# Hashed attention with a three-way maxout layer: weight tiles added by VectorE in three bursts of the first batch, the fourth pair's hash one unit earlier, and two end pieces

## The chip, the cores and the metric

One core of a Trainium2 chip runs the whole kernel. The metric is the device time of one launch in microseconds. Times inside the kernel are counted from the start of the profiled span.

## The reference, cut to what matters

```python
# q, k, v: 4 batches x 8 heads x 768 rows x 64; proj: 64 x 6
q_bucket = bucket of the 6 signs of q @ proj ; k_bucket likewise
scores = where(q_bucket[:, None] == k_bucket[None, :], 0.125 * q @ k.T, -1e9)
attn = exp(scores - max);  attn = attn / (sum(attn) + 1e-9);  x = attn @ v
# x: 3072 rows x 512 (the heads side by side)
h = maximum(maximum(x @ w1, x @ w2), x @ w3)      # 512 -> 768
out = h @ w_out                                   # 768 -> 512, float32
```

Each row's weights are divided by their sum. How that sum is formed is what the first part of the change touches.

## The kernel before, in words

**Units.** The work is cut into chunks of query rows: three of 256 rows in batch 0, two of 384 in each other batch, nine in all (0 to 8). A unit is a part of one chunk and one head: 768 scores per partition, three blocks of 256 or two of 384. A chunk and head has two units in batch 0 and three later, so each batch has 48 units. In batch 0 the order of units is: chunks 0, 1, 2 for head 0, the same for head 1, then heads 2 and 3 of each chunk in turn, then heads 4 to 7 of chunk 0 (units 24 to 31), of chunk 1 and of chunk 2.

For each unit, `scores` (line 289) issues TensorE matmuls of keys against queries (line 305) into one of two PSUM buffers, and one ScalarE exponential (line 313) into one of 24 weight tiles `AT`. Bits of the hash stand as extra rows of the matmul operand `S`, so that unequal buckets get a weight of almost nothing.

**Bursts.** A burst is one chunk and one half of the heads, written (chunk, half): (1, 0) is chunk 1 with heads 0 to 3. It has three pieces. `sums` (line 358) adds the weights over the keys: matmuls against a 128 x 32 matrix of ones (line 365), four heads side by side; VectorE turns the sums into reciprocals in four steps (lines 372 to 376, `ys`, `rr`, `rr`, `rb`). `values` (line 378) multiplies the weights with `v`, once for even and once for odd columns (line 387), and VectorE scales the result into `xT` (line 394). In chunks 3 to 8 VectorE first adds a head's weight tiles (`add`, line 329), so that fewer matmuls are needed in `sums`; in chunks 0 to 2 all six blocks of a head go through TensorE, 24 matmuls a burst.

**Order.** Nothing is left to a scheduler. Every engine runs its instructions in the order in which the program issues them, and waits where an operand or a buffer isn't there. The loop at line 624 issues, for unit `u`: the scores of unit `u + 1`, then whatever `when(u, ...)` has listed for `u`, then ffn steps as the credit allows, then pieces of bursts. The bursts of batch 0 have units of their own:

```python
u = {(0, 0): (16, 17, 20), (1, 0): (21, 22, 24), (2, 0): (26, 27, 29)}.get((c, i), (d, d, d))[n]
```

Burst (0, 1) has `d = 32` for its three pieces. The ffn of chunk 0 starts two units later; its first matmuls (line 420) need all of that chunk's `xT`.

**Hash.** For the heads of batch 0 by pairs: a transposing matmul (line 123), copies into `T`, GpSimd's scaled copy into `S` (line 137), the projection matmul, and VectorE's sign bits (line 153). For pairs 2 and 3 (`pair_hash`, line 145; pair 2 is the third and pair 3 the fourth) four small DMAs carry the bits into `S`: key side and query side of two heads. Pair 3 is hashed at unit 18; its key bits are sent by SyncE at once, its query bits by ScalarE's queue at unit 20. Pair 3 is first used by unit 28.

For later batches VectorE transposes four loaded heads (line 209), GpSimd narrows them to 16 bits (line 214), SyncE places them (line 219), and the hash (lines 228 to 239) sends its bits. The transposes of the first such group stand at units 22 to 29, one each.

**End.** The last block of 128 output rows is written in pieces, `last` (line 441): TensorE matmuls (line 445), a copy by ScalarE or VectorE (lines 449, 451), a DMA by that engine's queue or SyncE's (line 453).

Of the kernel before, what the change touches and what calls it, by code (L numbers as in the profile page):

```python
# [10 lines left out]
FP16 = mybir.dt.float16  # L11
BF16 = mybir.dt.bfloat16
AluOp = mybir.AluOpType
# [4 lines left out]
def kernel(  # L18
# [12 lines left out]
    nc = tc.nc  # L31
    B, H, S, D = q.shape
    NBITS = proj.shape[1]
    P = 128
    NM = S // P
    HALF = S // 2
    MH = NM // 2
    DM = H * D
# [14 lines left out]
    NAT = 24  # L53
    SPREAD = {2: (61, 9), 3: (100, 12)}
    THIRD_ADD = 5
    LAG = (1, 4)
    ATW = 776

# [8 lines left out]
    ad_pool = ctx.enter_context(tc.tile_pool(name="adpool", bufs=5))  # L67
# [22 lines left out]
    def bank():  # L90
        i = free_banks.pop(0)
        return i, bank_tiles[i]

    def give(i):
        if i is not None:
            free_banks.append(i)


    nat, t32, t16, s_of, where, v_at = {}, {}, {}, {}, {}, {}
# [42 lines left out]
        pair_keep(pi, side, hd, mp, eng)  # L142
        give(i)

    def pair_hash(pi, late=None):
        i, bp = bank()
        for side in (1, 0):
            for hd in range(2):
                g = 2 * side + hd
                nc.tensor.matmul(bp[Q * g : Q * (g + 1), 0:HALF], pj2[:, :],  # L150
                                 t32[pi][:, side, hd * HALF : (hd + 1) * HALF], start=True, stop=True)
        bits = b_pool.tile([P, HALF], BF16, tag="bits", name="bits")
        nc.vector.tensor_scalar(out=bits[:], in0=bp[:, 0:HALF], scalar1=0.0, scalar2=0.5,
                                op0=AluOp.is_gt, op1=AluOp.subtract)
        give(i)

        def send(eng, sides):
            for hd in range(2):
                for side in sides:
                    g = 2 * side + hd  # L160
                    eng.dma_start(s_of[pi][D : D + NBITS, g, :].rearrange("b (c n) -> b c n", c=2),
                                  bits[Q * g : Q * g + 2 * NBITS, :])

        if late:
            send(nc.sync, (1,))
            when(late, send, nc.scalar, (0,))
        else:
            send(nc.sync, (1, 0))


    def first_place(side, hd, par, mp):
# [101 lines left out]
    done_at = {}  # L273
# [8 lines left out]
    def blocks(t, w):  # L282
        nb = 2 * HALF // w
        return t[:, 0 : nb * (w + 2)].rearrange("p (n c) -> p n c", n=nb)

    def block_of(b, m):
        return 2 * (m % MH) + m // MH if b == 0 else m
# [29 lines left out]
    def weights_of(c, h, m):  # L317
        w = chunks[c][2]
        nb = 2 * HALF // w
        return blocks(at_tiles[at_of[unit_at[c, h, m // nb]]], w)[:, m % nb, :]  # L320

    def xt_of(c):
        if c not in xts:
            xts[c] = x_pool.tile([P, NJC, HALF], FP16, tag="xT", name="xT")
        return xts[c]

    sum_of = {}

    def add(c, h, n):
        w = chunks[c][2]  # L330
        t = [blocks(at_tiles[at_of[unit_at[c, h, i]]], w)[:, :, 0:w] for i in range(n + 1)]
        if n == 1:
            sum_of[c, h] = ad_pool.tile([P, 2, HALF], FP16, tag="ad", name="ad")
        else:
            t[0] = sum_of[c, h][:]
        nc.vector.tensor_tensor(out=sum_of[c, h][:], in0=t[0], in1=t[n], op=AluOp.add)  # L336
        if n == 2 and c >= THIRD_ADD:
            t = sum_of[c, h]
            nc.vector.tensor_tensor(out=t[:, 0, :], in0=t[:, 0, :], in1=t[:, 1, :], op=AluOp.add)  # L339

    def sum_blocks(c, h):
        w = chunks[c][2]
        if (c, h) in sum_of:
            t = sum_of[c, h]
            return [t[:, j, 0:w] for j in range(1 if c >= THIRD_ADD else 2)]
        return [weights_of(c, h, m)[:, 0:w] for m in range(NM)]

    def burst(c, i):
# [60 lines left out]
    def ffn_groups(c):  # L409
        b, q0, w = chunks[c]  # L410
        xt = xt_of(c)
        hts, gs, l2 = {}, [], {}
        jobs = [(fb, wi) for fb in range(NFB) for wi in range(3)]
        if c == 0:
            jobs = [(fb, wi) for wi in range(3) for fb in range(NFB)]
        for fb, wi in jobs:
            def go(fb=fb, wi=wi):
                k_, ps = bank()
                for jc in range(NJC):
                    nc.tensor.matmul(ps[:, 0:w], w_sb[wi][:, jc, fb * P : (fb + 1) * P], xt[:, jc, 0:w],  # L420
                                     start=(jc == 0), stop=(jc == NJC - 1))
                if wi == 0:
                    hts[fb] = h_pool.tile([P, HALF], FP16, tag="ht", name="ht")
                    if w == HALF:
                        nc.scalar.copy(hts[fb][:, 0:w], ps[:, 0:w])  # L425
                    else:
                        nc.vector.tensor_copy(hts[fb][:, 0:w], ps[:, 0:w])
                else:
                    nc.vector.tensor_tensor(out=hts[fb][:, 0:w], in0=hts[fb][:, 0:w], in1=ps[:, 0:w], op=AluOp.max)  # L429
                give(k_)  # L430
            gs.append(go)
        rows = out[b * S : (b + 1) * S, :].rearrange("(p c) m -> c p m", c=NM)

        def out_rows(tb):
            if c < NCH - 1:
                return o_pool.tile([P, DM], FP32, tag="osb", name="osb")
            if "end" not in nat:
                nat["end"] = nat_pool.tile([P, 4 * NM * D], FP32, tag="nat", name="nat")
            return nat["end"][:, tb * DM : (tb + 1) * DM]

        def last(tb, cs, use_act):
            k_, ps = bank()
            n = cs.stop - cs.start
            for fb in range(NFB):
                nc.tensor.matmul(ps[:, 0:n], hts[fb][:, tb * P : (tb + 1) * P], wout_sb[:, fb, cs],
                                 start=(fb == 0), stop=(fb == NFB - 1))
            osb = out_rows(tb)
            if use_act:
                nc.scalar.copy(osb[:, cs], ps[:, 0:n])
            else:  # L450
                nc.vector.tensor_copy(osb[:, cs], ps[:, 0:n])
            give(k_)
            (nc.scalar if use_act else nc.sync).dma_start(rows[block_of(b, q0 // P + tb)][:, cs], osb[:, cs])

        def item(tb, part):
            def go2(part, tb=tb):
                if c == NCH - 1 and tb == w // P - 1:
                    if part == 0:
                        last(tb, slice(0, DM // 2), False)
                    else:  # L460
                        last(tb, slice(DM // 2, 3 * DM // 4), True)
                        last(tb, slice(3 * DM // 4, DM), False)
                    return
                if part == 0:
                    l2[tb] = bank()
                k_, ps = l2[tb]
                for fb in range(part * MH, (part + 1) * MH):
                    nc.tensor.matmul(ps[:, 0:DM], hts[fb][:, tb * P : (tb + 1) * P], wout_sb[:, fb, :],  # L468
                                     start=(fb == 0), stop=(fb == NFB - 1))
                if part == 1:  # L470
                    osb = out_rows(tb)
                    nc.scalar.copy(osb[:, 0:DM], ps[:, 0:DM])  # L472
                    give(k_)
                    nc.sync.dma_start(rows[block_of(b, q0 // P + tb)], osb[:, 0:DM])
            gs.append(lambda: go2(part))

        ntb = w // P
        steps = [(0, 0)]
        for tb in range(1, ntb):
            steps += [(tb, 0), (tb - 1, 1)]  # L480
        steps.append((ntb - 1, 1))
        if c == NCH - 1:
            steps = steps[:-3] + [steps[-2], steps[-3], steps[-1]]
        for tb, part in steps:
            item(tb, part)
        return gs
# [3 lines left out]
    def when(u, f, *args):  # L490
        at.setdefault(u, []).append(lambda: f(*args))

    with tc.manual_schedule():
# [80 lines left out]
        when(9, t32.pop, 1)  # L574
        when(14, pair_hash, 2)
        when(15, t32.pop, 2)
        when(18, pair_hash, 3, 20)
        when(19, t32.pop, 3)
        when(17, load_v, 1)
        for n, u in ((1, 6), (2, 20), (3, 31)):  # L580
            when(u, load_weights, n)
# [4 lines left out]
        for g in range(2, NQUAD):  # L586
            b2, i2 = divmod(g, 2)
            need = UPB * b2 + 12 * i2
            for n, side in enumerate((1, 0)):
                name = (side, g)  # L590
# [17 lines left out]
        for c, i in sorted(done_at, key=lambda e: done_at[e]):  # L608
            d = done_at[c, i] + LAG[c > 2]
            sums, values = burst(c, i)  # L610
            pieces = [lambda f=sums: f(0, NM), lambda f=values: f(0, 0, NM), lambda f=values: f(1, 0, NM)]
            for n, f in enumerate(pieces):
                u = {(0, 0): (16, 17, 20), (1, 0): (21, 22, 24), (2, 0): (26, 27, 29)}.get((c, i), (d, d, d))[n]
# [6 lines left out]
        for u, (c, h, n) in enumerate(units):  # L620
            if c >= 3 and n:
                when(min(u + 2, NU - 1), add, c, h, n)

        for u in range(NU):
            if 0 < u < NU - 1:
# [55 lines left out]
```

## Time and profile before

| what | value |
|---|---|
| median of 3 runs | 265.78 us (265.35 to 266.68) |
| the profiled execution | 265.72 us, span 263.3 us |
| TensorE matmul, weight load | 256.2 us (97%), 154.2 us (59%) |
| VectorE, ScalarE, GpSimd | 208.4 us (79%), 177.4 us (67%), 69.9 us (27%) |
| TensorE's granted clock | 1.0 |
| sums without adds (line 365, 128 x 256) | 144 matmuls, 24 in each burst |
| adds of two weight tiles (line 336) | 48, mean 545 ns |

A timeline line gives start and length in microseconds, the engine, line and operation, output and inputs, shapes, how many instructions are merged in it, and in brackets the idle time before it with what ended it. A `q` behind an engine's name means its queue issues a DMA. A line of busy times by stretch gives the stretch, its length, then for TensorE, weight load, VectorE, ScalarE and GpSimd the busy time and number of instructions, then the granted clock, DMA share and GB/s. A group of instructions has its busy time, the mean length in ns and the idle time before it. Lines refer to the kernel as shown.

### The profile page before, as it was taken

What the parts mean: (1) busy time and instruction counts of PE and PEld (TensorE: products, weight loads), DVE (VectorE), ACT (ScalarE), POOL (GpSimd) and SP (SyncE); (2) the same over time, 40 slices, a digit from 0 to 9 for tenths busy, and PEclk for the clock granted to TensorE, in tenths of its full rate; (3) what the DMA queues carried; (4) which work ended last, traced back from release to release, by engine and by line L of the source; (5) the groups of instructions that cost most, each with busy time, mean ns of one, the idle gap of its engine ahead of it and who ended that gap; (6) DMA issues with size and microseconds to landing.
All of it is one profiled execution on the core that took longest, in us unless ns stands there. A gap on an engine that the chain in (4) does not pass through costs nothing.

```text
span 263.3 us, 6497 instructions
## 1 busy us (share of the span) xinstructions
PE 256.2 (97%) x2509; PEld 154.2 (59%) x2509; DVE 208.4 (79%) x494; ACT 177.4 (67%) x257; POOL 69.9 (27%) x132
## 2 busy tenths in 40 slices
PE   7999999999999999999999999999999999999994
PEld 3555658866765666555555554655555555554552
DVE  3897767967799999969999996999859795887451
ACT  3697785667968675956869588584886859581322
POOL 5587752355043526330141612011000000000000
PEclk9999999999999999999999999999999999999999
DMA  6998999869732964970063753802030003000303
GB/s 199 301 247 176 193 256 236 167 118 209 191 91 65 207 143 62 267 185 21 0 193 108 121 120 52 206 0 70 7 123 0 0 2 121 2 0 2 120 0 120
DMA packets 20861, 30.95 MB, mean 118 GB/s; under 512 B 2624, under 2 KB 15392, under 8 KB 20832
## 3 DMA queue, kind: packets, MB, share of 16 engines
q0 software_dynamic: 8128, 13.37, 27.0%
q1 hardware_dynamic: 12156, 16.71, 21.8%
q10 hardware_dynamic: 548, 0.48, 0.7%
q8 instruction: 19, 0.31, 0.5%
q14 instruction: 10, 0.08, 0.1%
HBM read 25.17 MB, written 6.29 MB: 119 GB/s over the span
## 4 chain that ended last, share of the span: by engine, by line
PE 84%; DVE 7%; POOL 3%; issue 1%; DMA 1%; ACT 1%; ACTq 0%; DVEq 0%
PE ms L420 34%; PE sc L305 21%; PE ms L468 11%; PE ms L387 9%; PE ms L228 3%; PE ms L365 2%; POOL S L137 2%; DMA nat<-in_q_dram 1%; DVE S L183 1%; PE ms L123 1%; PE ms L178 1%; DVE ht L429 1%; DVE T L132 1%; DVE ad L336 1%; DVE xT L394 1%
## 5 line engine op out<-in xcount | busy, mean ns | idle before, releaser
L313 ACT ACTIVATE AT<-sc 128x768 f16<-128x768 f32 x192 | 152.7, 816 | 59.6 <-PE sc L305 54.9
L420 PE MATMUL ms<-xT,w_sb 128*128 128x384 f16 (+1 forms) x648 | 115.0, 307 | 0.3 <-DVE xT L394 0.2
L305 PE MATMUL sc<-S 72*128 72x384 bf16 (+1 forms) x432 | 93.9, 308 | 1.6 <-ACT AT L313 0.7
L420 PEld LDWEIGHTS <-w_sb 128*128 128x128 f16 x648 | 62.7, 97 | 35.9 <-issue 0.4
L429 DVE TENSOR_TENSOR ht<-ht,ms 128x384 f16<-128x384 f16 (+1 forms) x108 | 54.2, 503 | 20.8 <-PE ms L420 10.3
L305 PEld LDWEIGHTS <-S 72*128 72x128 bf16 (+1 forms) x432 | 39.4, 98 | 32.7 <-issue 11.9
L214 POOL TENSOR_SCALAR T<-T 128x768 bf16<-128x768 f32 x24 | 22.9, 952 | 90.3 <-issue 48.3
L468 PE MATMUL ms<-wout_sb,ht 128*128 128x512 f16 x138 | 35.5, 378 | 0.0
L387 PE MATMUL ms<-AT,vo 128*32 128x385 f16 (+3 forms) x840 | 34.3, 308 | 0.0
L387 PEld LDWEIGHTS <-vo 128*32 128x32 f16 x864 | 22.9, 96 | 9.2 <-issue 1.7
L336 DVE TENSOR_TENSOR ad<-ad,AT 128x768 f16<-128x768 f16 x48 | 26.5, 552 | 2.1 <-ACT AT L313 1.3
L209 DVE STREAM_TRANSPOSE T<-nat 128x384 f32<-128x384 f32 x48 | 26.8, 563 | 0.0
L336 DVE TENSOR_TENSOR ad<-AT,AT 128x768 f16<-128x768 f16 x48 | 26.2, 545 | 0.2 <-ACT AT L313 0.2
L425 ACT CAST ht<-ms 128x384 f16<-128x384 f32 x36 | 17.3, 480 | 8.1 <-PE ms L420 8.1
L468 PEld LDWEIGHTS <-ht 128*128 128x128 f16 x138 | 13.3, 97 | 13.0 <-issue 0.3
L394 DVE SCALAR_TENSOR_TENSOR xT<-ms,sv,rb 128x384 f16<-128x384 f32 (+1 forms) x35 | 19.2, 566 | 1.4
L472 ACT COPY osb<-ms 128x512 f32<-128x512 f32 x21 | 12.3, 587 | 7.1 <-PE ms L468 5.8
L339 DVE TENSOR_TENSOR ad<-ad 128x384 f16<-128x384 f16 x32 | 15.5, 485 | 1.1
L137 POOL TENSOR_SCALAR S<-T 64x384 bf16<-64x384 f32 (+1 forms) x23 | 14.2, 617 | 5.8 <-DVE T L132 4.3
L203 POOL DMA_DIRECT2D nat<-in_q_dram x20 | 11.1, 560 | 0.1
L372 DVE STREAM_TRANSPOSE ys<-ms 128x384 f32<-128x384 f32 (+1 forms) x17 | 9.0, 530 | 2.4 <-PE ms L365 2.3
L183 DVE TENSOR_SCALAR S<-ms 6x384 bf16<-6x384 f32 x16 | 8.9, 554 | 2.4 <-PE ms L178 2.0
(52 smaller groups left out, 122.0 us busy)
## 6 DMA issues: line engine op xcount, KB each, us to landing
out_dram<-osb SPq DMA_DIRECT2D x21, 256.0 KB
S<-T SPq DMA_DIRECT2D x48, 96.0 KB
nat<-in_q_dram POOLq DMA_DIRECT2D x20, 192.0 KB, 6.4
vo<-in_v_dram POOLq DMA_DIRECT2D x8, 384.0 KB, 6.1
nat<-in_k_dram POOLq DMA_DIRECT2D x16, 192.0 KB, 5.8
w_sb<-in_moe_w_dram POOLq DMA_DIRECT2D x3, 768.0 KB, 12.0
nat<-in_k_dram SPq DMA_DIRECT2D x10, 192.0 KB
nat<-in_k_dram SPq DMA_DIRECT2D x3, 384.0 KB
```

The lines of the kernel that those rows point to most:

```text
L137: nc.gpsimd.tensor_scalar(out=o, in0=i_, scalar1=RS, scalar2=1.0, op0=AluOp.mult, op1=AluOp.mult)
L209: nc.vector.transpose(t32[name][:, u, half * HALF : (half + 1) * HALF], i_)
L214: nc.gpsimd.tensor_scalar(out=t16[name][:, u, :], in0=t32[name][:, u, :], scalar1=RS, scalar2=1.0, op0=AluOp.mult, op1=AluOp.mult)
L305: nc.tensor.matmul(views[j], s_of[kn][0 : D + bits, kx, m * P : (m + 1) * P], s_of[qn][0 : D + bits, qx, q0 : q0 + w], start=True, stop=True)
L313: nc.scalar.activation(t[:, :, 0:w], whole, ActFn.Exp, bias=-SCALE * 0.25 * bits, scale=SCALE)
L336: nc.vector.tensor_tensor(out=sum_of[c, h][:], in0=t[0], in1=t[n], op=AluOp.add)
L387: nc.tensor.matmul(av[Q * x : Q * (x + 1), 0:n], v_at[2 * b + i][:, x, cb * D + side : (cb + 1) * D : 2], weights_of(c, 4 * i + x, m)[:, 0 ...
L394: nc.vector.scalar_tensor_tensor(out=xt_of(c)[:, 2 * i + side, 0:w], in0=av[:, 0:w], scalar=sv_of[b, i, side][:], in1=rb[0][:, 0:w], op0=A ...
L420: nc.tensor.matmul(ps[:, 0:w], w_sb[wi][:, jc, fb * P : (fb + 1) * P], xt[:, jc, 0:w], start=(jc == 0), stop=(jc == NJC - 1))
L425: nc.scalar.copy(hts[fb][:, 0:w], ps[:, 0:w])
L429: nc.vector.tensor_tensor(out=hts[fb][:, 0:w], in0=hts[fb][:, 0:w], in1=ps[:, 0:w], op=AluOp.max)
L468: nc.tensor.matmul(ps[:, 0:DM], hts[fb][:, tb * P : (tb + 1) * P], wout_sb[:, fb, :], start=(fb == 0), stop=(fb == NFB - 1))
```

## The change

Three edits. VectorE adds the two weight tiles of each head in the bursts (1, 0), (2, 0) and (0, 1): twelve adds more, and 12 instead of 24 matmuls in the sums of each of the three. The adds stand at units 17, 17, 19, 20 for (1, 0), ahead of its sums at 21; at 22, 22, 23, 24 for (2, 0), ahead of 26; at 27, 29, 31, 32 for (0, 1), ahead of 32. In a unit, an add comes behind the transpose of that unit and ahead of a burst's pieces. The fourth pair's hash moves from unit 18 to 17, which puts its matmuls ahead of the values of (0, 0) instead of behind block 19, and all four of its bit DMAs go to SyncE. The last output block is written in two pieces of 256 columns (ScalarE's copy and queue, then VectorE's copy and SyncE's queue) instead of pieces of 256, 128 and 128 (VectorE, ScalarE, VectorE).

```diff
+    ADDED = ((1, 0), (2, 0), (0, 1))
+    ADD_FROM = {(0, 1): 17, (0, 2): 22, (1, 0): 0, (1, 1): 0, (1, 2): 0}
...
-    def pair_hash(pi, late=None):
+    def pair_hash(pi):
...
-        def send(eng, sides):
-            for hd in range(2):
-                for side in sides:
-                    g = 2 * side + hd
-                    eng.dma_start(s_of[pi][D : D + NBITS, g, :].rearrange("b (c n) -> b c n", c=2),
+        for hd in range(2):
+            for side in (1, 0):
+                g = 2 * side + hd
+                nc.sync.dma_start(s_of[pi][D : D + NBITS, g, :].rearrange("b (c n) -> b c n", c=2),
                                   bits[Q * g : Q * g + 2 * NBITS, :])
-
-        if late:
-            send(nc.sync, (1,))
-            when(late, send, nc.scalar, (0,))
-        else:
-            send(nc.sync, (1, 0))
...
         if n == 1:
-            sum_of[c, h] = ad_pool.tile([P, 2, HALF], FP16, tag="ad", name="ad")
+            ad = ad_pool.tile([P, 2, HALF], FP16, tag="ad", name="ad").rearrange("p a c -> p (a c)")
+            sum_of[c, h] = ad.rearrange("p (n c) -> p n c", c=w)
         else:
-            t[0] = sum_of[c, h][:]
-        nc.vector.tensor_tensor(out=sum_of[c, h][:], in0=t[0], in1=t[n], op=AluOp.add)
+            t[0] = sum_of[c, h]
+        nc.vector.tensor_tensor(out=sum_of[c, h], in0=t[0], in1=t[n], op=AluOp.add)
...
-            return [t[:, j, 0:w] for j in range(1 if c >= THIRD_ADD else 2)]
+            return [t[:, j, :] for j in range(1 if c >= THIRD_ADD else 2 * HALF // w)]
...
                 if c == NCH - 1 and tb == w // P - 1:
-                    if part == 0:
-                        last(tb, slice(0, DM // 2), False)
-                    else:
-                        last(tb, slice(DM // 2, 3 * DM // 4), True)
-                        last(tb, slice(3 * DM // 4, DM), False)
+                    last(tb, slice(part * DM // 2, (part + 1) * DM // 2), part == 0)
                     return
...
-        when(18, pair_hash, 3, 20)
-        when(19, t32.pop, 3)
+        when(17, pair_hash, 3)
+        when(18, t32.pop, 3)
...
             if c >= 3 and n:
                 when(min(u + 2, NU - 1), add, c, h, n)
+            if (c, h // 4) in ADDED and n:
+                when(min(max(u + 2, ADD_FROM[h // 4, c]), done_at[c, h // 4] + 1), add, c, h, n)
```

## The prediction

> **What bounds the kernel now.** I read the page first: busy times and the chain that ended last.
>
> ```profile
> PE 256.2 (97%) x2509; PEld 154.2 (59%) x2509; DVE 208.4 (79%) x494; ACT 177.4 (67%) x257; POOL 69.9 (27%) x132
> PE 84%; DVE 7%; POOL 3%; issue 1%; DMA 1%; ACT 1%; ACTq 0%; DVEq 0%
> ```
>
> TensorE carries 84% of the chain, so its work looks worth removing. But the change lies in one stage, and the span's shares say nothing of it. Hence the busy times of the stretch with the three changed bursts, then its timelines, TensorE first.
>
> ```profile
> 29.00:41.00 12.00, 11.31 (x221) 7.22 (x221) 8.82 (x22) 9.07 (x12) 5.95 (x12) 1.00 1.08 226
> ```
> ```profile
> 28.18 0.84 PE L365 MATMUL ms<-AT,ones 128*32 128x256 f16 x24
> 33.01 0.85 PE L365 MATMUL ms<-AT,ones 128*32 128x256 f16 x24
> 37.99 0.49 PE L305 MATMUL sc<-S 70*128 70x256 bf16 x3 [0.34 <-ACT AT L313]
> 39.73 0.84 PE L365 MATMUL ms<-AT,ones 128*32 128x256 f16 x24
> 40.39 1.52 PE L387 MATMUL ms<-AT,vo 128*32 128x257 f16 x48
> 43.19 0.27 PE L420 MATMUL ms<-xT,w_sb 128*128 128x256 f16 x1 [0.19 <-DVE xT L394]
> ```
>
> The L365 rows are the sums that the change halves. After 43.19 the next row with a wait is at 81.36 (0.14 us), so what is late at 43.19 is late at the end. That row waits for VectorE. VectorE's timeline:
>
> ```profile
> 30.00 0.45 DVE L376 STREAM_TRANSPOSE rb<-rr 128x256 f32<-128x256 f32 x1
> 30.37 0.54 DVE L209 STREAM_TRANSPOSE T<-nat 128x384 f32<-128x384 f32 x1
> 30.83 0.44 DVE L394 SCALAR_TENSOR_TENSOR xT<-ms,sv,rb 128x256 f16<-128x256 f32 x1
> 31.19 1.02 DVE L209 STREAM_TRANSPOSE T<-nat 128x384 f32<-128x384 f32 x2
> 33.91 0.45 DVE L372 STREAM_TRANSPOSE ys<-ms 128x256 f32<-128x256 f32 x1 [0.22 <-PE ms L365]
> 39.98 0.56 DVE L231 TENSOR_SCALAR bits<-ms 128x384 bf16<-128x384 f32 x1 [2.56 <-PE ms L228]
> 40.61 0.45 DVE L372 STREAM_TRANSPOSE ys<-ms 128x256 f32<-128x256 f32 x1
> ```
>
> From 29.07 to 40.61 VectorE is idle only 0.22 + 2.56 = 2.78 us. That is all the cover the adds have there. Last, ScalarE at the moved DMA issues, then a place where an add meets GpSimd:
>
> ```profile
> 27.13 1.42 ACTq L161 DMA_DIRECT2D S<-bits  x1
> 28.59 0.74 ACTq L161 DMA_DIRECT2D S<-bits  x1
> 29.38 3.17 ACT L313 ACTIVATE AT<-sc 128x768 f16<-128x768 f32 x4 [1.13 <-PE ms L365]
> ```
> ```profile
> 84.63 0.51 DVE L336 TENSOR_TENSOR ad<-AT,AT 128x768 f16<-128x768 f16 x1
> 85.25 0.99 DVE L336 TENSOR_TENSOR ad<-ad,AT 128x768 f16<-128x768 f16 x1
> ```
> ```profile
> 84.86 0.99 POOL L214 TENSOR_SCALAR T<-T 128x768 bf16<-128x768 f32 x1 [2.55 <-issue]
> ```
>
> The second add starts while GpSimd narrows and ends 0.40 after it (85.84 to 86.24), 0.44 longer than its group's 0.55. The narrowing that met the first add took 0.99, not 0.83.
>
> **The change, part by part.** Times below are starts. "Block n" is the score matmuls of unit n; a burst is (chunk, half of the heads).
>
> *Fourth hash one unit earlier.* Today values of (0,0) lie between blocks 18 and 19 and the hash between 19 and 20; afterwards both lie between 18 and 19. A score block ahead of another kind takes 0.43 (23.76 to 24.20), values 0.78 (24.20 to 24.98), the hash 0.78 (25.42 to 26.20). Block 19 then starts at 25.76, not 24.98; its exponential 0.54 later (24.98 to 25.52 today) and 0.81 long, to 27.11. Block 21 needs the score buffer that this frees (there are two): 27.16, not 26.54. Sums (1,0) follow at 28.80, not 28.18: **+0.62**.
>
> *Sums halved.* 24 matmuls take 0.66 (39.73 to 40.39); 12 fewer save **0.33** a burst. After sums (1,0) TensorE is 0.29 late, and VectorE's first step of that burst is at 29.36 instead of 29.07.
>
> *Query-side bits to SyncE.* ScalarE loses two issues. Exponential 22 starts at 28.91 instead of 29.38 and block 24 no longer waits (0.21 today). TensorE is at 30.49 there against 30.44: level again. SyncE gets two issues of 0.72; its four now run from about 26.0 to 29.0, after the third pair's end at 25.95. The loads queued behind start at 29.0 instead of 28.54, and their transposes only at 45.37. The bits are issued 0.3 earlier than the last is today, and block 28 needs them first, at 33.80. Nothing for either.
>
> *Adds of (1,0).* Four adds of 0.47 from start to start (62.83 to 63.30) and the earlier bits fit between 25.2 and 28.3, ahead of sums (1,0) at 28.80. Free; two meet GpSimd's S narrowing (26.67 to 28.39), which brings the last to 28.8. No margin remains.
>
> *Adds of (2,0).* They go between transposes. From 29.36: the reciprocal's four steps 1.30 (29.07 to 30.37), transpose 0.48, two adds 0.94, xT 0.39, transpose 0.48, add 0.47, transpose 0.48: the last add starts at 33.90 and is done at 34.40. Sums (2,0) are in TensorE's order and wait to 34.45; today 33.01. Everything behind them on TensorE waits. Less 0.33, block 28 starts at 34.89, not 33.80.
>
> *Adds of (0,1).* VectorE runs on without a gap: xT 34.37, two transposes, the reciprocal's steps from 35.72 to 37.02, then transpose, add, xT, two transposes, add, xT, two adds (0.48 + 0.47 + 0.39 + 0.96 + 0.47 + 0.39 + 0.94 = 4.10) to 41.12. The last add is done at 41.15; sums (0,1) start at 41.20, end 0.56 later, and L372 starts at 41.76 instead of 40.61. L420 follows at the same distance: **+1.15**. As a cross-check, eight adds cost 3.76, less the 2.78 of cover, plus the 0.29 late start: 1.27.
>
> *Meetings with GpSimd.* Two of the four narrowings of this stretch each run into a second add, by the order of transposes and adds: the last add of (2,0) ends at 34.55 instead of 34.40 (the narrowing ends at 34.15, plus 0.40), and the third of (0,1) about 0.25 later: **+0.4**. Bounds: 0, or four full meetings at 0.44 = 1.8. I take 0.4, the count from the order.
> The Trainium skill (SBUF — State Buffer, section "SBUF: two separate sides") says VectorE operations with two SBUF inputs and GpSimd share a port pair as an exclusive lock, the loser blocking fully. By that rule a narrowing that meets an add would also wait for its end and then take its whole 0.83; the two meetings would cost 0.26 more, 0.66 in all. The traced 0.99 is below that, and I keep 0.4.
>
> *The end.* Twelve matmuls of 128 columns become six of 256; starts 0.055 and 0.11 apart, so TensorE ends alike (259.73). VectorE's last copy is 256 wide, 0.42 instead of 0.29 (rows of 259.10 and 259.84), but starts 0.07 sooner, as it waits for no ScalarE copy: +0.06. The last DMA has 1024-byte packets of 46 ns instead of 512-byte ones of about 29 ns, eight per engine: +0.1. Together **+0.15** (0.05 to 0.3).
>
> Sum: 1.15 + 0.4 + 0.15 = **+1.7**. The profiled execution took 265.72 (span 263.3 and 2.42 around it), 0.06 under the median of 265.78; so 267.4 for it and **267.5** as a median. Unsure: an add at 0.44 or 0.55 from start to start (8 x -0.03 = -0.25, 8 x 0.08 = +0.65), the first step (0 to 0.62, worth up to 0.55 at the end), the meetings (0 to 1.8).
>
> **Rivals.** Half a per cent, about what a measurement of this kernel can tell from no change, is 1.33 us here.
>
> *Mostly hidden (same).* Without the hash's stall and without meetings, VectorE starts the stretch on time: 0.67 late at 43.19, plus the end, +0.8; with adds at 0.44, +0.5. Result 265.6 to 266.9, at about 266.4. For it: 2.56 us of VectorE's idle lie just ahead of the last sums. Against: sums (2,0) come before that idle.
>
> *Faster, by TensorE.* If the adds always finish before their sums, TensorE loses 3 x 0.33 = 1.0, and without the ScalarE issues its waits at 30.44, 37.16 and 37.99 go (0.21 + 0.12 + 0.34 = 0.7): -1.7 + 0.15, or 264.2. It decides if the last add of (2,0) is done by 33.0. For it: TensorE's 97%. Against: eight adds, 3.76, stand against 2.78 of idle, and L420 at 43.19 already waits for VectorE.
> The Trainium skill (Perfetto Trace Analysis, "Identifying the Most-Contended Engine") wants TensorE judged by weight loading and other engines by occupancy. Here 59% stands against VectorE's 79%, so it too speaks against this rival.
>
> *Slower still, by the port.* Every narrowing meets a second add: 1.8 instead of 0.4, +3.1, or 268.8. For it: adds that follow a transpose meet the narrowing released by that transpose, as at 84.86. Against: behind two of the four stand xT or ys, not adds.
>
> **How the numbers follow.** The forecast (VectorE full from 29.4 to 44, +1.0 to +2.6) gets 0.62, mostly hidden 0.26, faster 0.05, the port 0.07. Of the forecast's 0.62, 0.07 lies below +1.33. So slower 0.55 + 0.07 = 0.62, same 0.26 + 0.07 = 0.33, faster 0.05. The range 265.6 to 268.7 takes in the forecast and nearly all of mostly hidden; the faster case and most of the port are left out, about 0.13.
>
> **What would show it.** VectorE without an idle gap from the first changed reciprocal to the ffn; a TensorE wait for VectorE ahead of the L365 rows of (2,0), about 1.4 us, and of (0,1), some 0.2 to 0.5; ScalarE without the gap at 28.25; the first ffn matmul that waits about 1.6 later than 43.19; the shift kept to the end. I am wrong if the sums of (2,0) start by 33.3 or the shift shrinks after the ffn begins.

## The result, and the profile after

The changed kernel took 268.63 us (median of 11 executions, 267.56 to 272.2), the kernel before 265.85 us beside it. The ratio is 1.0089 [1.0068, 1.0109]: slower by 0.9%, where the prediction said 267.5 us (265.6 to 268.7). The ratio leaves out three executions of the changed kernel, of 271.93 to 272.2 us with TensorE's mean clock at 0.981; the two medians, which keep them, stand at 1.0105.

The profile below is that of a second run of the same kernel (e1_after: 269.96 us, span 268.0), because TensorE was at half clock for three times as long in the first one's. Its first TensorE wait for an exponential is at 20.37 us, in the profile of before at 19.71; so a time of it stands 0.66 lower "by before's clock", and the other runs are set against before in the same way. Line 365 is now 361, 305 is 300, 336 is 332, 372 is 368, 394 is 390, 420 is 416, 209 is 204, 214 is 209, 472 is 464.

Busy times, then the engines' shares of the chain that ended last:

```profile
PE 258.0 (96%) x2467; PEld 154.1 (58%) x2467; DVE 214.4 (80%) x505; ACT 177.5 (66%) x257; POOL 70.8 (26%) x132
...
PE 82%; DVE 9%; DMA 3%; ACT 2%; issue 2%; POOL 1%; ACTq 0%; DVEq 0%
```

VectorE has 6.0 us more and stands in more of the chain, as forecast. DMA at 3% instead of 1% was not. Next the stretch with the three bursts, 29.00 to 41.00 by before's clock:

```profile
29.66:41.66 12.00, 10.40 (x150) 5.84 (x151) 11.76 (x30) 7.82 (x11) 6.05 (x12) 0.86 1.00 217
```

VectorE (the fourth time in the line) is busy for 11.76 of 12.00 us, against 8.82; TensorE (the second) for 10.40 against 11.31. The granted clock behind the counts is 0.86 instead of 1.00. TensorE's timeline of that stretch:

```profile
34.46 0.27 PE L361 MATMUL ms<-ad,ones 128*32 128x256 f16 x1 [0.18 <-DVE ad L332]
35.56 0.80 PE L361 MATMUL ms<-ad,ones 128*32 128x256 f16 x9 [0.83 <-DVE ad L332]
...
46.69 0.27 PE L416 MATMUL ms<-xT,w_sb 128*128 128x256 f16 x1 [0.32 <-DVE xT L390]
```

The sums of (2, 0) begin at 33.33 by before's clock (33.99), wait twice for an add, 0.18 + 0.83 us, and get on at 34.90. The nine matmuls behind the wait take 0.80 us, not the 0.49 that nine take in another run below: that is the lower clock. VectorE and GpSimd beside it:

```profile
30.31 0.45 DVE L368 STREAM_TRANSPOSE ys<-ms 128x256 f32<-128x256 f32 x1
...
34.82 0.69 DVE L332 TENSOR_TENSOR ad<-AT,AT 128x768 f16<-128x768 f16 x1
...
41.09 1.26 DVE L332 TENSOR_TENSOR ad<-AT,AT 128x768 f16<-128x768 f16 x2
```
```profile
34.13 0.96 POOL L209 TENSOR_SCALAR T<-T 128x768 bf16<-128x768 f32 x1 [2.26 <-DVE T L204]
```

VectorE has no gap from the first changed reciprocal at 30.31 to the last add. The last add of (2, 0) runs on 0.42 past the end of the narrowing that it met (35.09 to 35.51) and takes 0.69 us, where others take 0.52.

The rest of the loss is far from the change. First a ScalarE row of before near the end; then, of e1_after, the chain, TensorE's timeline and the same ScalarE row:

```profile
244.97 0.58 ACT L472 COPY osb<-ms 128x512 f32<-128x512 f32 x1 [0.83 <-DMA out_dram<-osb]
```
```profile
246.37 3.92 DMA out_dram<-osb
```
```profile
251.03 5.20 PE L416 MATMUL ms<-xT,w_sb 128*128 128x384 f16 x31 [1.46 <-ACT osb L464]
```
```profile
250.39 0.58 ACT L464 COPY osb<-ms 128x512 f32<-128x512 f32 x1 [2.75 <-DMA out_dram<-osb]
```

A store of chunk 7 takes 3.92 us from issue to landing, 2.0 in the kernel before (242.87 to 244.87). The third copy of that chunk needs its buffer (there are two) and waits 2.75 us instead of 0.83; TensorE stands still for 1.46 us until 251.03.

### The profile page after: what moved, and what is told of

Read it like the earlier page. It is cut to its first block, busy times and chain, and to the rows that moved or that the text cites. A ratio compares the mean times of both kernels' runs of the same rounds, so it can differ in the third digit from the quotient of the medians.

```text
span 270.2 us, 6423 instructions
## 1 busy us (share of the span) xinstructions
PE 260.4 (96%) x2467; PEld 154.8 (57%) x2467; DVE 214.5 (79%) x505; ACT 177.7 (66%) x257; POOL 70.9 (26%) x132
## 4 chain that ended last, share of the span: by engine, by line
PE 83%; DVE 8%; DMA 3%; issue 2%; ACT 2%; POOL 1%; DVEq 0%; ACTq 0%
PE ms L416 32%; PE sc L300 21%; PE ms L460 10%; PE ms L383 10%; PE ms L223 4%; PE ms L361 2%; DVE ad L332 2%; DMA S<-bits 2%; DMA out_dram<-osb 2%; DVE S L178 1%; ACT AT L308 1%; PE ms L508 1%; PE ms L125 1%; DVE ht L425 1%; PE ms L173 1%
## 5 line engine op out<-in xcount | busy, mean ns | idle before, releaser
L300 PE MATMUL sc<-S 72*128 72x384 bf16 (+1 forms) x432 | 95.5, 314 | 2.0 <-ACT AT L308 1.2
L300 PEld LDWEIGHTS <-S 72*128 72x128 bf16 (+1 forms) x432 | 40.2, 99 | 33.6 <-issue 12.7
L209 POOL TENSOR_SCALAR T<-T 128x768 bf16<-128x768 f32 x24 | 23.5, 978 | 92.4 <-issue 48.2
L383 PE MATMUL ms<-AT,vo 128*32 128x385 f16 (+3 forms) x840 | 35.5, 316 | 0.0
L332 DVE TENSOR_TENSOR ad<-AT,AT 128x768 f16<-128x768 f16 x60 | 33.4, 561 | 0.8 <-ACT AT L308 0.8
```

The lines of the kernel that those rows point to most:

```text
L209: nc.gpsimd.tensor_scalar(out=t16[name][:, u, :], in0=t32[name][:, u, :], scalar1=RS, scalar2=1.0, op0=AluOp.mult, op1=AluOp.mult)
L300: nc.tensor.matmul(views[j], s_of[kn][0 : D + bits, kx, m * P : (m + 1) * P], s_of[qn][0 : D + bits, qx, q0 : q0 + w], start=True, stop=True)
L332: nc.vector.tensor_tensor(out=sum_of[c, h], in0=t[0], in1=t[n], op=AluOp.add)
L383: nc.tensor.matmul(av[Q * x : Q * (x + 1), 0:n], v_at[2 * b + i][:, x, cb * D + side : (cb + 1) * D : 2], weights_of(c, 4 * i + x, m)[:, 0 ...
```

## The experiments

**e1_after**: the changed kernel again.

> The changed kernel again, to have its profile with the granted clock at 1.0 throughout. VectorE full (the forecast's theory): +1.7 us against before, the sums of (2,0) wait to about 34.5, the first ffn matmul that waits stands near 44.7, and the shift is the same from there to the end. Clock theory (a stall of about 1 us ahead of the sums of (2,0) lets TensorE's granted clock fall): executions with a mean clock below 1.0 among those with 1.0, and +2.4 or more in the median.

Measured 269.54 (six executions, 267.77 to 271.9), 1.0106 [1.0074, 1.0138]. Over both runs of this kernel, 8 of 17 executions had a mean granted clock of 0.999 or more and took 267.56 to 268.63; 4 had 0.993 or 0.994, up to 269.96; 5 had 0.981 and took 271.8 to 272.2. This is the pattern that the clock theory expected, lower clocks among full ones and more than +2.4 us. No profile of the kernel at full clock came of it.

**e2_adds_only**: the kernel before with the twelve adds alone.

```diff
+    ADDED = ((1, 0), (2, 0), (0, 1))
...
+            if (c, h // 4) in ADDED and n:
+                when(min(max(u + 2, ADD_FROM[h // 4, c]), done_at[c, h // 4] + 1), add, c, h, n)
```

> Before, with the twelve adds alone (fourth hash at unit 18, query bits on ScalarE's queue, three end pieces). VectorE full with meetings: +1.6 us, nearly all of the change. VectorE full without meetings: +0.7. TensorE bound (rival): -1.0.

Measured 269.14 (267.3 to 270.07), 1.0117 [1.0085, 1.0149]. The adds alone cost what the whole change costs, as far as six executions tell, and about twice the +1.6 that was expected: the lower clock and the late wait for a store (4.15 us from issue to landing) are in this kernel too. Without the hash's delay the sums of (1, 0) wait as well (the first row).

```profile
29.13 0.49 PE L368 MATMUL ms<-ad,ones 128*32 128x256 f16 x9 [0.59 <-DVE ad L339]
...
34.90 0.49 PE L368 MATMUL ms<-ad,ones 128*32 128x256 f16 x9 [0.83 <-DVE ad L339]
```

**e3_hash_only**: hash at unit 17 and all of its bits on SyncE, nothing else.

```diff
-            when(late, send, nc.scalar, (0,))
...
-        when(18, pair_hash, 3, 20)
+        when(17, pair_hash, 3)
```

> Before, with the fourth pair's hash at unit 17 and its four bit DMAs on SyncE, no adds. VectorE full: block 21 waits for exponential 19, sums (1,0) 0.6 later; the ScalarE issues that are gone give some of it back, so +0.35 at the first ffn matmul and in the time. TensorE bound (rival): -0.7, as the waits of TensorE for ScalarE at 30.4, 37.2 and 38.0 go.

Measured 266.57 (265.68 to 267.9), 1.0022 [1.0006, 1.0038]. The wait at block 21 is 0.57 us; the ffn's first waiting matmul stands at 43.42 by before's clock, against 43.19: most of the delay is gone by then, about 0.2 stays. The time rose by 0.6 us, by its interval 0.2 to 1.0, where 0.35 was expected.

**e4_end_only**: the two end pieces alone.

```diff
...
-                        last(tb, slice(DM // 2, 3 * DM // 4), True)
-                        last(tb, slice(3 * DM // 4, DM), False)
+                    last(tb, slice(part * DM // 2, (part + 1) * DM // 2), part == 0)
```

> Before, with two end pieces of 256 columns. Forecast: +0.15 us, all of it behind 259.1, the last TensorE matmul at the same place. If instead fewer pieces help (one copy and one DMA less): -0.1 to -0.3.

Measured 265.28 (264.89 to 267.93), 0.9979 [0.9952, 1.0007]. The span ends 3.13 us after the last matmul, before 3.57: a gain of 0.44 in the trace, more than either expectation had; the times alone don't settle it.

**e5_half_sums**: lighter sums without adds.

```diff
+            if (c, i) in HALVED:
+                bs = [blk[0:3] for blk in bs]
...
-                nc.vector.tensor_scalar(out=rr[:, 0:n], in0=ys[:, 0:w:Q], scalar1=EPS * S, scalar2=None, op0=AluOp.add)
+                nc.vector.tensor_scalar(out=rr[:, 0:n], in0=ys[:, 0:w:Q], scalar1=1.0 if (c, i) in HALVED else EPS * S, scalar2=None, op0=AluOp.add)
```

> The kernel before, with the sums of the three bursts taken over three of their six blocks (12 matmuls instead of 24 each) and no adds; this leaves half of those weights out of the sums, and nothing else. It asks what TensorE's lighter sums are worth alone, and where the late wait for a store comes from. If VectorE's adds cost what the prediction said, the sums alone give back at most 3 x 0.33 = 1.0 us in the first batch and no wait ahead of sums (2, 0); without anything late that is 264.9 to 265.5. If the late wait comes from the place of the instruction fetch, which 72 TensorE instructions fewer move later, this kernel shows a wait of ScalarE's L464 copy for the chunk-7 store of 2 to 3 us and a TensorE gap of 1.2 to 1.9 us near 247 to 251 although no add is in it: 266.2 to 267.0. If the late wait comes from the adds (from lateness, or from VectorE), there is none: 264.9 to 265.5. Clock: 1.0 throughout by every theory, since no wait of about 1 us is left in the first batch.

The kernel leaves half of the weights out of these sums, and it adds 1.0 to them in place of a small constant, which the expectation doesn't say; the instruction that adds it is otherwise the same.

Measured 266.61 (265.93 to 267.5), 1.0026 [1.0, 1.0051]. Less work on TensorE, no add, and yet not faster: the late wait is there. And the lighter sums are worth little by themselves. The first waiting ffn matmul stands at 43.10, or 43.02 by before's clock, against 43.19:

```profile
43.10 0.27 PE L423 MATMUL ms<-xT,w_sb 128*128 128x256 f16 x1 [0.32 <-DVE xT L397]
```

Of the 1.0 us that the three bursts could give back, 0.17 arrive there; the rest goes into longer waits on the way (0.56 us for GpSimd instead of 0.21, and a new one of 0.28 for an exponential). So the sums' share of the rival "faster, by TensorE" isn't there even without the cost of adds; e3 has shown the same of its other share, the ScalarE issues. Now the late wait: the chain, and one of the DMA queues from 242.77 to 247.20 (packets, MB, share of the DMA engines' time):

```profile
242.77 4.38 DMA out_dram<-osb
```
```profile
q8 instruction: 1, 0.02, 2.8%
```

This queue is not one of the kernel's own; the profile calls it that of the instructions. It carries packets of 16,384 bytes, 9 to 17 us apart in before from 95.7 to 240.3 us; between two of them TensorE executes some 250 matmuls and weight loads on average. So I take a packet for a fetch of instructions. In every profile the slow store goes with the place of that packet. Where the packet starts 0.9 us after the first store of chunk 7 (the changed kernel, e2, e5, e7, e9), 15 of the store's 16 semaphore increments have come 2.0 us after its issue, and the last comes after 3.9 to 4.4 us, or 3.3 in e7 and e9. Where it starts 1.4 to 2.6 us ahead of the store (before, e3, e4, e6, e8, e10 to e12), all 16 have come after 2.0. With 72 TensorE instructions fewer (36 matmuls and their weight loads) the packet comes at a later place of the program. So the wait needs no add and no lateness; that the number of TensorE's instructions sets it is what e6 tries.

**e6_after_dummy**: the changed kernel with TensorE's instructions restored.

```diff
+            if (c, i) in ADDED:
+                for m in range(3):
+                    for x in range(4):
+                        nc.tensor.matmul(sm[Q * x : Q * (x + 1), 0:w], ones[:, :], weights_of(c, 4 * i + x, m)[:, 0:w],
+                                         start=(m == 0), stop=(m == 2))
```

> The changed kernel with 12 matmuls more in each of the three bursts, of the weights that were not yet waited for by the adds, written to the same PSUM rows ahead of the real sums and overwritten by them; TensorE has its 24 matmuls a burst again, VectorE its adds. If the late wait comes from the place of the instruction fetch, it goes (TensorE has the old number of instructions up to there), no gap over 0.5 us near 250: -1.5 against the changed kernel. If it comes from being late, it stays. If the clock falls because TensorE stands still for about 1 us ahead of sums (2, 0), the dummies, 0.66 long, cut that wait to about 0.3 to 0.4, and the clock stays at 1.0 in all executions; if it falls for another reason (the adds themselves), it falls here too. The matmuls lie in TensorE's waits where there is one (2, 0) and cost up to 0.33 in the other two. By the fetch and the stall together: 266.3 to 267.2 (before +1.2 to +1.6 for VectorE, -0.44 for the end). By VectorE alone with neither: 268.5 to 269.5, as the changed kernel.

Measured 266.77 (266.23 to 268.29), 1.0035 [1.0008, 1.0062]: 36 matmuls more make the kernel faster by 1.9 us than it was without them, and by 1.2 us than its executions at full clock (median 267.96). The late wait is gone and the clock is 0.998 or more in all 12 executions, as the theories of the fetch and of the clock expected. The wait for the add was not cut to 0.4, though: it is one of 0.83 us.

```profile
35.36 0.49 PE L366 MATMUL ms<-ad,ones 128*32 128x256 f16 x9 [0.83 <-DVE ad L332]
...
45.29 0.27 PE L421 MATMUL ms<-xT,w_sb 128*128 128x256 f16 x1 [0.18 <-DVE xT L395]
```

With the clock at 1.0 this shows VectorE's delay undisturbed: 45.29 is 44.77 by before's clock (0.52 off), 1.58 late. By the times it is 266.77 less 265.85, plus the 0.44 that the end gives: 1.4.

**e7_after_nat7**: chunk 7's rows in a tile of their own.

```diff
-            if c < NCH - 1:
+            if c < NCH - 2:
...
-            if "end" not in nat:
-                nat["end"] = nat_pool.tile([P, 4 * NM * D], FP32, tag="nat", name="nat")
-            return nat["end"][:, tb * DM : (tb + 1) * DM]
+            if ("end", c) not in nat:
+                nat["end", c] = nat_pool.tile([P, 4 * NM * D], FP32, tag="nat", name="nat")
+            return nat["end", c][:, tb * DM : (tb + 1) * DM]
```

> The changed kernel, with chunk 7's output rows written into a tile of their own, so that the L464 copies of chunk 7 wait for no earlier store. If the late wait is that of a copy for the buffer that a slow store still reads, TensorE's gap near 251 goes, whatever makes the store slow: -1.5 against the changed kernel, 267.5 to 268.2 in the median, 266.4 to 266.8 in the executions at full clock; the slow store itself (about 4 us from issue to landing) still shows. If the gap comes from something else (TensorE's own instruction stream stopping for the fetch), it stays and the time is that of the changed kernel.

Measured 267.65 (266.23 to 270.37), 1.007 [1.003, 1.011]. The five executions at a clock of 0.998 or more took 266.23 to 266.73, median 266.5; the changed kernel's eight have a median of 267.96. So 1.5 us were the copy's wait for its buffer, and the gap of 1.46 is gone, though the store is still slow (3.3 us). Three executions at 0.994 took 267.6 to 267.84, four at 0.98 took 270.11 to 270.37: the lower clock costs about 1.2 or 3.7 us in these.

**e8_after_no20**: the changed kernel without the adds of (2, 0).

```diff
-    ADDED = ((1, 0), (2, 0), (0, 1))
+    ADDED = ((1, 0), (0, 1))
```

> The changed kernel without the adds of (2, 0): adds for (1, 0) and (0, 1) only, 24 matmuls again in the sums of (2, 0). The prediction laid the first of the two delays, 34.45 against 33.01 at sums (2, 0), on these four adds (1.88 us of VectorE). If that holds, TensorE waits at most 0.2 there, block 28 is on time, and VectorE's idle 2.6 us ahead of the last sums take up the four adds of (0, 1) but for 0.3: first batch +0.1 to +0.4 instead of +1.2 to +1.6. If the clock falls by the stall of about 1 us, it stays at 1.0 here. With 48 TensorE instructions fewer the fetch lies 2.3 us later than before instead of 3.5: the late wait may be there or not (0 to +1.5). Sum 265.5 to 267.1, the lower end without the late wait. If the delay were the number of adds over the whole stretch and not their place, the first batch would still lose 0.8 to 1.1 and the time be 266.2 to 268.0. If the clock falls for another reason, 0.7 to 1.7 more.

Measured 265.10 (264.67 to 265.84), 0.9964 [0.9941, 0.9988]: faster than both kernels, by 0.75 us against before, and the fastest that was run. That is also 0.4 below the range that was expected. No wait for an add, no lower clock, no late wait.

```profile
39.69 0.51 PE L361 MATMUL ms<-ad,ones 128*32 128x256 f16 x12
...
42.98 0.27 PE L416 MATMUL ms<-xT,w_sb 128*128 128x256 f16 x1 [0.32 <-DVE xT L390]
```

42.98 is 43.27 by before's clock: 0.08 late. With the four adds of (2, 0) gone, VectorE's delay is gone; those of (0, 1) fit into its idle time. But the adds that are left gain nothing either: the last matmul ends 0.07 us later than in before (by before's clock; 0.12 in e10, where the hash stays), and the span ends 3.13 us after it instead of 3.57. So by the trace e8's gain is that of the end pieces, which alone gave 265.28 (e4).

**e9_late_sums20**: e7 with the sums of (2, 0) two units later.

```diff
-(2, 0): (26, 27, 29)}
+(2, 0): (28, 28, 29)}
```

> The changed kernel with chunk 7's rows in a tile of their own, and with the sums and the first values of (2, 0) at unit 28 (from 26 and 27): two more score blocks stand ahead of those sums on TensorE. The adds stay where they are. If the early delay is the place of these sums (TensorE standing still for four adds in its order), it goes: no wait over 0.3 us there, the ffn's first waiting matmul within 0.3 of before's 43.19 (by the first exponential's wait as origin), 264.9 to 265.6. If VectorE is simply full between the first changed reciprocal and the ffn, the wait moves to the sums of (0, 1), whose adds end where they ended (some 41.6 by before's clock, against 39.73): first waiting ffn matmul still 0.9 to 1.3 late, 266.2 to 266.8. The clock stays at 1.0 in all executions by either, unless a single wait comes near 1 us again.

Measured 267.16 (eight executions, 266.44 to 267.83), 1.0042 [1.0026, 1.0058]. The clock is 0.998 or more in all of them, and nothing is won against e7's 266.5: the wait goes to the sums of (0, 1), as the theory of a full VectorE said, and the ffn is 1.79 late (45.53, less 0.55), more than its 0.9 to 1.3. VectorE's last add ends at 41.83 by before's clock, in e1_after at 41.69: VectorE's work ends at about the same time, wherever TensorE waits for it. Part of TensorE's delay is new, though: with the sums moved it waits 0.55 and 0.63 us for exponentials (before, 0.34 once).

```profile
41.97 0.27 PE L361 MATMUL ms<-ad,ones 128*32 128x256 f16 x1 [0.59 <-DVE ad L332]
42.43 0.49 PE L361 MATMUL ms<-ad,ones 128*32 128x256 f16 x9 [0.20 <-DVE ad L332]
...
45.53 0.27 PE L416 MATMUL ms<-xT,w_sb 128*128 128x256 f16 x1 [0.18 <-DVE xT L390]
```

**e10_two_bursts**: adds for (1, 0) and (0, 1) and the two end pieces on the kernel before, the hash as before.

> The kernel before with adds for (1, 0) and (0, 1) and the two end pieces; the fourth hash stays at unit 18 with its query bits on ScalarE's queue. Against e8 it tells what the moved hash does. By the prediction's working the moved hash delays TensorE by 0.62 at block 21, and without it sums (1, 0) come at 28.2 and wait for their adds instead, as in the run with adds alone (0.59): no difference from e8, 264.8 to 265.4. If the adds of (1, 0) are in time, or only the hash costs, it is 0.4 to 0.6 faster than e8, 264.5. If ScalarE's two issues hurt more than block 21's wait, slower, 265.6 to 266.0.

Measured 265.29 (265.01 to 265.83), 0.9983 [0.9971, 0.9995]; e8 has 265.10. The sums of (1, 0) wait 0.59 for an add, as expected: the hash's earlier place and that wait come out alike.

**e11_end_lane**: e4 with one output store of chunk 3 cut in two, so that there are 177 DMAs again.

```diff
+                    if c == 3 and tb == 0:
+                        nc.sync.dma_start(rows[block_of(b, q0 // P + tb)][:, 0 : DM // 2], osb[:, 0 : DM // 2])
+                        nc.sync.dma_start(rows[block_of(b, q0 // P + tb)][:, DM // 2 : DM], osb[:, DM // 2 : DM])
+                        return
```

> The kernel before with the two end pieces, and one output store of chunk 3 cut into two halves on the same queue, so that the program has 177 DMAs as before. If the end gains because the last store falls on the semaphore that SyncE waits for last, the extra store moves it to the first in that list again: seven more waits behind it, 0.4 us between its landing and the end of the list, span end 3.5 to 3.6 after the last matmul, 265.6 to 265.9. If the gain comes from the pieces themselves, it stays: 3.1, 265.2 to 265.4.

Measured 266.37 (265.08 to 268.43), 1.0014 [0.9992, 1.0035]: too wide to settle it by time. The trace does: the span ends 3.57 us after the last matmul again, with the two pieces in place. The last rows of TensorE and their spans, e4 first, then e11 (start, length, and "span" at the head of the same answer; to two places the spans are 262.98 and 263.64):

```profile
core 0 of [0], span 263.0 us
...
258.38 1.47 PE L445 MATMUL ms<-wout_sb,ht 128*128 128x256 f16 x12
```
```profile
core 0 of [0], span 263.6 us
...
258.60 1.47 PE L445 MATMUL ms<-wout_sb,ht 128*128 128x256 f16 x12
```

Why seven of its twelve executions took over 266.3 stays open.

**e12_one_burst**: adds for (0, 1) alone and the two end pieces.

> The kernel before with adds for (0, 1) alone and the two end pieces; hash as before. Its four adds have VectorE's 2.56 us of idle time just ahead of those sums. If adds are free where they fit into idle time, TensorE gains 0.33 in that burst and 0.44 at the end: 264.9 to 265.1, no wait for an add. If the ffn's first waiting matmul is bound by VectorE anyway (its wait of 0.19 grows), the sums' gain is lost: 265.2 to 265.4, as with the end pieces alone. With 24 TensorE instructions fewer ahead of it the late fetch should still fall clear of chunk 7's store.

Measured 265.64 (264.97 to 268.59), 0.9995 [0.9972, 1.0019]: nothing can be told of the time. But its profiled execution (267.88 us) is a case of the lower clock without any add near it. A transposing matmul of the hash waited for VectorE's copy. TensorE's timeline, and then two stretches of 3.41 us (granted clock behind the five engines):

```profile
21.92 0.52 PE L125 MATMUL ms<-iden,nat 128*128 128x128 f32 x3 [0.99 <-DVE T L134]
```
```profile
19.00:22.42 3.42, 2.10 (x21) 1.36 (x22) 2.74 (x6) 2.82 (x4) 1.71 (x3) 1.00 1.12 206
22.42:25.83 3.41, 3.41 (x18) 1.53 (x17) 1.63 (x3) 0.81 (x1) 3.25 (x6) 0.50 0.59 121
```

The same stretches of e1_after, and then the one of e6 that holds its wait:

```profile
32.11:35.53 3.42, 2.31 (x35) 1.24 (x34) 3.42 (x9) 2.92 (x4) 0.96 (x1) 1.00 1.21 257
35.53:38.94 3.41, 3.38 (x39) 1.71 (x39) 3.31 (x10) 0.81 (x1) 1.13 (x2) 0.50 1.07 237
```
```profile
33.71:37.12 3.41, 2.58 (x55) 1.52 (x54) 3.38 (x9) 1.89 (x3) 1.80 (x2) 1.00 1.11 253
```

The clock changes are 3.413 us or a multiple of it apart in every profile, so these stretches can be laid out from the changes (for e6, which has none here, from the clock's first record of that launch). TensorE was idle for 1.32 us in the stretch ahead of e12's drop, 1.10 ahead of e1_after's, 0.98, 1.14 and 1.15 in e2's, the first profile's and e7's; for 0.83 in e6 and 0.79 in e9, without a drop. So around these waits of the first batch the drop goes with TensorE's idle time within one such stretch, 0.98 us or more against 0.83 or less, and not with the adds. (It isn't this change's alone: e4 had one execution of twelve at 0.992, and the kernel before one at 0.981, 271.52 us.)

Idle time is not all that counts, though. The late wait leaves TensorE idle for as long and longer without a drop. The first profile's stretch with it, and the next one:

```profile
249.96:253.37 3.41, 1.55 (x10) 0.84 (x9) 0.00 (x0) 0.76 (x2) 0.00 (x0) 1.00 0.22 82
253.37:256.78 3.41, 3.41 (x22) 2.05 (x21) 2.23 (x5) 1.17 (x3) 0.00 (x0) 1.00 0.20 77
```

That is 1.86 us of idle time and a clock of 1.00 behind it; e2 and e5 have 1.69 and 1.61 there, e1_after 0.99, and none drops. Nor did the clock fall behind the first such stretch of e4, from 4.74 us, with 1.04 us. The matmuls around the late wait are all 128*128, while in the first batch many are 128*32 or 70*128; whether that makes the difference, no run tells.

The Trainium skill (TensorE: Matmul & The Clock Gate, section "Part 1: The HAM clock gate") has this window of 3413 ns and says that it runs free of the kernel; here the trace agrees. It gives one idle window as what halves the clock; here about a third of one was enough in the first batch, and over half of one was not near the end. That the wait falls into one stretch in some executions and across two in others would explain why only 9 of 17 executions of the changed kernel slowed down; that part is argued, since no profile shows an execution of it at full clock.

## Why the prediction was right, and where it was wrong

Against 265.85, the changed kernel's executions at full clock (267.96) are 2.1 us late. By e7 that is made of VectorE's delay, about +1.1 (266.5 less 265.85, plus the 0.44 of the end), the late wait +1.5 and the end -0.44; by e6 of +1.4, +1.2 and -0.44. The lower clock in half of the executions lifts the median to 268.63. The forecast had +1.7 from other parts: 1.55 for VectorE and 0.15 for the end.

- **VectorE full: right.** Its idle time in the stretch fell from 3.18 to 0.24 us, TensorE waits ahead of the sums of (2, 0) (1.0 us, where about 1.4 was forecast), and the shift is kept to the end (in e1_after, with the lower clock, 2.84 us at the ffn and 2.84 at chunk 7's first copy). The sums of (2, 0) get on at 34.90 by before's clock (forecast 34.45, with the meeting about 34.6): VectorE's first step came at 29.65, not 29.36. The ffn's first wait moves by 1.58 in e6, forecast 1.55; the times say 1.1 (e7) to 1.4 (e6). e9 shows that it is the sum of VectorE's work that binds: the wait moved, VectorE's last add and the loss stayed.
- **The second delay, of (0, 1): wrong in its place.** In e6 block 28 starts 1.46 late, and TensorE needs the same 5.93 us from there to the next changed burst as in before. The loss is whole at (2, 0); TensorE loses only about 0.1 more at (0, 1), whose adds take up what VectorE had left of idle time.
- **Sums halved, 0.33 each: right for (0, 1)** (0.32 instead of 0.66 us to the next row in e8), next to nothing for (1, 0), whose sums wait for the last add; and e5 shows that without adds only 0.17 of the three times 0.33 reaches the ffn.
- **The hash, 0.62: right** (0.57 at block 21), but not level again: e3 keeps 0.24.
- **Meetings with GpSimd, 0.4: right.** The adds at 34.82 and 41.09 take 0.17 and 0.28 more than without: 0.45. By the rule of the Trainium skill (SBUF — State Buffer, section "SBUF: two separate sides"), as the prediction worked it out, it would have been 0.66. The sum is nearer to 0.4, but the order of the rows is the rule's. The three narrowings that met an add (at 34.13, 38.64 and 40.42) ended 0.68, 0.69 and 0.69 us after that add, and the add at 34.82 ended 0.42 after its narrowing. So each waits for the other; only the whole 0.83 behind the add, which the prediction put in, isn't there.
- **The end, +0.15: wrong in sign, -0.44.** The prediction added up a longer copy and longer packets. SyncE sees the last store landed 2.23 us after the last matmul in before and 2.22 in e4, so pieces and packets cost nothing. But SyncE then waits for a list of eight semaphores in a fixed order, 0.06 us each; the stores take the semaphores in turn. In before the last store has the first of them, and seven waits still follow; with one DMA fewer it has the last. e11 put one DMA back, and the 0.44 was lost.
- **Not in the sum: the late wait (+1.5) and the lower clock.** The working treated 36 matmuls fewer as time saved where they stood, and a wait of 1.4 us as its own length. The first moved an instruction fetch into a store on which a copy waits; the second halved the clock for 3.4 us or more behind it. Both come from side effects for which the profile of before has rows (the instruction queue, the granted clock) but shows no case.

So the sign and the main mechanism held. That the time came within 1.2 us is partly luck: the end was sized 0.6 too high and VectorE up to 0.4, against 1.2 to 1.5 us of late wait and a lower clock that were not in it. The median of 268.63 lies just below the upper bound of 268.7, and that of the second run of the same kernel (269.54) above it.

## What to carry to other kernels

Before work is moved to an engine "with idle time", count that time in the stretch where the work has to be done. Eight adds (3.76 us) against 2.78 us of idle time cost TensorE 1.4 us (e7's 266.5 against e8's 265.1), and moving the wait (e9) did not help; the four with the idle time just ahead of their sums cost about nothing. They also gained nothing: a lighter load on TensorE pays only where TensorE isn't then kept waiting by another engine (e5). When instructions are removed, see which transfers the instruction fetches will meet afterwards, and give a copy that stands behind a store a buffer of its own. A wait can cost more than its length: here one of 1.0 us in the first batch went with a lower TensorE clock in 9 of 17 executions, and with matmuls of no use in part of it (e6) that was gone in all twelve.

## What the runs showed of the hardware that was not expected

- Between 19 and 45 us TensorE's clock fell to 0.50 for 3.41 or 10.24 us after 0.98 to 1.32 us of idle time in one stretch of 3.41 us, and did not after 0.83. Near the end it did not fall after 0.99 to 1.86 us. What else counts is open.
- An instruction fetch, one packet of 16,384 bytes and 0.9 to 2.0 us long, that starts 0.9 us after a 256 KB store delays the last of the store's 16 increments from 2.0 to between 3.3 and 4.4 us after issue; the other 15 come as before.
- A VectorE add and a GpSimd narrowing that met it waited for each other: the narrowing ended 0.68 or 0.69 us after the add, the add behind it 0.42 us after the narrowing.
- SyncE's closing waits make the end of the kernel depend on how many DMAs were issued before: 3.57 or 3.13 us after the last matmul, by the count of one.
